# Second product of a Strassen feed-forward kernel transposed: weight sums stationary, 512 tokens moving

## The chip, the cores and the metric

The kernel runs on one core of one Trainium2 chip. The metric is the device time of one execution in microseconds. The engines that matter are TensorE (PE for matmuls, PEld for loading the stationary operand), VectorE (DVE), ScalarE (ACT) and SyncE (SP), which issues nearly all DMAs from one queue, in order.

## The reference

A retention layer (linear attention with a decaying state) feeds a two-layer network without bias:

```
state = gamma * state + k_t outer v_t;   y_t = q_t . state / sqrt(64)      # 4 batches, 8 heads, 768 steps
x = y as [3072 tokens, 512]
h = x @ w_in                # [3072, 2048]
g = h * clip(h + 3, 0, 6) / 6
out = g @ w_out             # [3072, 512]
```

All arrays are 32-bit floats. Each matmul operand is split into a high part in the reduced format fp32r and a low remainder, and a product takes three matmuls: high times high, high times low, low times high.

## The kernel before

The first part computes the retention and the first product, six groups of 512 tokens (u = 0 to 5) by sixteen pieces of the inner dimension of 128 each (jj). Its matmuls (L335) keep a 128x128 piece of w_in stationary and move 512 tokens, so h comes out transposed, inner dimension on the partitions. ACT (L339) and DVE (L340) make g, and SP writes it to arrays gd in the chip's main memory (L341), one array for each pair of inner pieces, 256 KB a time.

The second part is g @ w_out by one level of Strassen's method, in Winograd's form: seven products instead of eight. The quadrants of g are the two halves of a group of 256 tokens by the two halves of the inner dimension. For each of twelve groups (tb), four chunks (cf) of the inner dimension load the four quadrants (L398, two DMAs of 256 KB), DVE makes four sums of 128x256 (L86, L89), and `split` makes the high parts on ACT (L133) and the remainders on DVE (L134), seven operands together, held in `gc`. The sums of w_out, `w2c`, are made once, during the first part. The matmuls (L421) keep a 128x128 piece of `gc` stationary and move 256 columns of `w2c`; the seven products stand in four banks of the accumulator memory. At a group's end a chain of seven additions (L436) combines them into `ot`, which SP stores.

Raw quadrants (`gr`) have four buffers and `gc` four, two of each in either of two pools. TensorE's order in the first part is written by hand; in the second part, and on all other engines, a planner orders the instructions by its own estimate of when each can run, and queues then run strictly in that order. The first chunk's loads and splits have high priority; the other chunks of the first group may not be issued before the first part's last g.

Of the kernel before, what the change touches and what calls it, by code (L numbers as in the profile page):

```python
# [9 lines left out]
F32 = mybir.dt.float32  # L10
F32R = mybir.dt.float32r
# [3 lines left out]
AF = mybir.ActivationFunctionType  # L15
ALU = mybir.AluOpType
# [3 lines left out]
P = 128  # L20
SIXTH = 1.0 / 6.0

LEFT = {1: 0, 2: 1, 3: 2, 4: 3, 5: 4, 6: 5, 7: 6}
RIGHT = {1: 0, 2: 1, 3: 2, 4: 3, 5: 4, 6: 5, 7: 6}


# [1 line left out]
def retention_ffn(ctx: ExitStack, tc: tile.TileContext, qkv, w_in, w_out, dvs, dqs, out, B, H, S, D):  # L30
# [4 lines left out]


    nc = tc.nc
    NT, DM = out.shape
    NF = w_in.shape[0]
    NFP = NF // 2  # L40
    NPAIR = H // 2
# [3 lines left out]
    UR = 4  # L45
    UT = UR * P
    NU = NROW // UR
    HM = DM // 2
    WARM = 14
    AHEAD = 2 * UR  # L50
    WITH = (0, 2, 3, 5)
# [4 lines left out]
    NSLOT = 10  # L56
# [4 lines left out]
    dram = ctx.enter_context(tc.tile_pool(name="dram", bufs=1, space=DRAM))  # L61
    wpool = ctx.enter_context(tc.tile_pool(name="wpool", bufs=NSLOT))

    gd = [dram.tile([P, 2, NT], F32, name=f"gd{j}") for j in range(NFP)]

    cst_sb = const.tile([P, ROWS_B, H], F32, name="cst_sb")
    nc.scalar.dma_start(out=cst_sb.rearrange("p n h -> p (n h)"), in_=dvs)
# [5 lines left out]
        out=mask, in_=mask, pattern=[[1, P]], compare_op=ALU.is_ge, fill=0.0, base=0, channel_multiplier=-1  # L73
# [58 lines left out]
    def split(hi, lo, src):  # L132
        nc.scalar.activation(out=hi, in_=src, func=AF.Copy)  # L133
        nc.vector.tensor_tensor(out=lo, in0=src, in1=hi, op=ALU.subtract)  # L134
# [24 lines left out]
    w2c = {}  # L159
# [26 lines left out]
    xs, rows, before, early = {}, {}, {}, {}  # L186
# [143 lines left out]
    def mm1(u, jj):  # L330
        h = ps_h.tile([P, UT], F32, tag="h", name=nm("h"))
        for k in range(NK):
            t, o = w1_block(jj, k)
            for n, (a, b) in enumerate(((0, 0), (0, 1), (1, 0))):
                nc.tensor.matmul(  # L335
                    h, t[:, o, a], xs[u][b][:, k], start=k + n == 0, stop=(k, n) == (NK - 1, 2), skip_group_check=True
                )
        g = hpool.tile([P, UT], F32, tag="g", name=nm("g"))
        nc.scalar.activation(out=g, in_=h, func=AF.Relu, bias=three)  # L339
        ins = nc.vector.scalar_tensor_tensor(out=g, in0=g, scalar=6.0, in1=h, op0=ALU.min, op1=ALU.mult)  # L340
        nc.sync.dma_start(out=gd[jj // 2][:, jj % 2, u * UT : (u + 1) * UT], in_=g)  # L341
# [29 lines left out]
    ph1.close()  # L371


    sets = (late, ctx.enter_context(tc.tile_pool(name="gcpool", bufs=1, reuse_waits="tile")))
    gpool = ctx.enter_context(tc.tile_pool(name="gpool", bufs=2, reuse_waits="tile"))
    ps_o = [
        ctx.enter_context(tc.tile_pool(name=f"ps_o{i}", bufs=1, space=PSUM, reuse_waits="tile", side=side))
        for i, side in enumerate(("right", "left"))
    ]
    CF = 2  # L380

    for tb in range(NT // (2 * P)):
        t0 = tb * 2 * P
        banks = [ps_o[tb % 2].tile([P, 512], F32, tag=f"o{i}", name=f"o{tb}_{i}") for i in range(4)]
        acc = {}
        for b_, ids in enumerate(((1, 2), (6, 7), (5, 3), (4,))):
            for n, i in enumerate(ids):
                acc[i] = (banks[b_][:, n * HM : (n + 1) * HM], n == 0)
        for cf in range(NFP // CF):
            pool = sets[cf % 2]  # L390
            with ExitStack() as first:
                if tb == 0 and cf < 1:
                    first.enter_context(tc.high_priority())
                elif tb == 0:
                    first.enter_context(tc.issue_after(end))
                gv = pool.tile([P, CF, 2, 2, P], F32, tag="gr", name=f"gr{tb}_{cf}", bufs=2)
                for jj in range(CF):
                    nc.sync.dma_start(  # L398
                        out=gv[:, jj].rearrange("p f t n -> p f (t n)"),
                        in_=gd[cf * CF + jj][:, :, t0 : t0 + 2 * P],  # L400
                    )
                a11, a12, a21, a22 = gv[:, :, 0, 0, :], gv[:, :, 1, 0, :], gv[:, :, 0, 1, :], gv[:, :, 1, 1, :]
                sm = pool.tile([P, 4, CF, P], F32, tag="gsum", name=f"gsum{tb}_{cf}")
                dve_add(sm[:, 1], a21, a22)
                dve_sub(sm[:, 2], sm[:, 1], a11)
                dve_sub(sm[:, 3], a11, a21)
                dve_sub(sm[:, 0], a12, sm[:, 2])
                gc = pool.tile([P, 2, 7, CF, P], F32R, tag="gc", name=f"gc{tb}_{cf}")
                for i, src in ((0, a11), (1, a12), (3, a22)):
                    split(gc[:, 0, i], gc[:, 1, i], src)  # L410
                split(gc[:, 0, 4:7], gc[:, 1, 4:7], sm[:, 1:4])
                split(gc[:, 0, 2], gc[:, 1, 2], sm[:, 0])
            order = [(jj, i) for jj in range(CF) for i in (1, 2, 6, 7, 5, 3, 4)]
            if t0 + 2 * P == NT and cf == NFP // CF - 1:
                order.sort(key=lambda ji: (1, 2, 6, 7, 5, 3, 4).index(ji[1]))
            for jj, i in order:
                j = cf * CF + jj
                wc = w2c[j]
                ps, first = acc[i]
                for n, (a, b_) in enumerate(((0, 0), (0, 1), (1, 0))):  # L420
                    nc.tensor.matmul(  # L421
                        ps,
                        gc[:, a, LEFT[i], jj, :],
                        wc[:, RIGHT[i], b_],
                        start=first and j == 0 and n == 0,
                        stop=j == NFP - 1 and n == 2,
                        skip_group_check=True,
                    )
        ot = gpool.tile([P, 2, DM], F32, tag="ot", name=f"ot{tb}")
        p1 = gpool.tile([P, HM], F32, tag="op1", name=f"op1_{tb}")  # L430
        u2 = gpool.tile([P, HM], F32, tag="ou2", name=f"ou2_{tb}")
        u3 = gpool.tile([P, HM], F32, tag="ou3", name=f"ou3_{tb}")
        u4 = gpool.tile([P, HM], F32, tag="ou4", name=f"ou4_{tb}")

        def acc6(out_, i, other, s=SIXTH):
            nc.vector.scalar_tensor_tensor(out=out_, in0=acc[i][0], scalar=s, in1=other, op0=ALU.mult, op1=ALU.add)  # L436

        nc.scalar.activation(out=p1, in_=acc[1][0], func=AF.Copy, scale=SIXTH)
        acc6(ot[:, 0, :HM], 2, p1)
        acc6(u2, 6, p1)  # L440
        acc6(u3, 7, u2)
        acc6(ot[:, 1, HM:], 5, u3)
        acc6(u4, 5, u2)
        acc6(ot[:, 0, HM:], 3, u4)
        acc6(ot[:, 1, :HM], 4, u3, -SIXTH)
        rows = out[t0 : t0 + 2 * P, :].rearrange("(t p) m -> p t m", p=P)
        if t0 + 2 * P < NT:
            nc.sync.dma_start(out=rows, in_=ot)
# [63 lines left out]
```

## Time and profile before

| | us |
|---|---|
| median of 3 runs | 609.75 (608.75 to 611.29) |
| profiled execution: its own time is given as its span, first to last instruction | 608.6 |
| first matmul of the second product | 365.05 |
| last matmul starts | 604.65 |
| matmuls of the first product (128x512 moving) | 1152 |
| matmuls of the second product (128x256 moving) | 2016 |
| DMA traffic over the span | 104.07 MB |

The rows of a group read: line, engine, operation, output and inputs, shape, count, then busy time and mean duration of one, then the idle time before them and who ended it. Matmuls overlap in the pipeline, so the time that one costs is read from the distance of many starts, not from its duration.

### The profile page before, as it was taken

The numbers are of one execution on the slowest core, as the hardware profiler recorded it, in microseconds if no ns is written. First come the engines' busy times: TensorE is split into PE (matmuls) and PEld (weight loads), VectorE is DVE, ScalarE is ACT, GpSimd is POOL, SyncE is SP. The second block draws the span as 40 slices with busy tenths as digits, with TensorE's granted clock in tenths as the row PEclk, the third lists the DMA queues.
The fourth block names the chain that finished last, engine by engine and source line by source line (L and its number), as shares of the span: only waits on it lengthen the run. The fifth ranks groups of instructions, "written<-read, shape, count | busy, mean of one in ns | idle before, by whom it ended". The sixth has DMA issues, their size and how long they took to land.

```text
span 608.6 us, 11524 instructions
## 1 busy us (share of the span) xinstructions
PE 594.1 (98%) x4444; PEld 536.7 (88%) x4444; DVE 457.5 (75%) x960; ACT 258.6 (42%) x540; POOL 20.1 (3%) x24
## 2 busy tenths in 40 slices
PE   7699999999999999999999999999999999999997
PEld 6586888888888888888888889999999999999997
DVE  4879999999333596333336979988898889988983
ACT  6764454544222353222224544444444444444441
POOL 0001000000100010000000000000000000000000
PEclk9989999999999999999999999999999999999999
DMA  8965677666644467455334426443444344434411
GB/s 324 389 234 191 226 248 260 207 209 225 217 164 156 156 208 258 148 165 173 124 122 155 173 97 198 139 127 117 139 139 139 105 139 139 139 104 140 143 66 36
DMA packets 64728, 104.07 MB, mean 171 GB/s; under 512 B 5793, under 2 KB 30881, under 8 KB 64673
## 3 DMA queue, kind: packets, MB, share of 16 engines
q1 hardware_dynamic: 64528, 103.31, 50.7%
q8 instruction: 35, 0.57, 0.4%
q14 instruction: 21, 0.16, 0.1%
q10 hardware_dynamic: 144, 0.02, 0.0%
HBM read 71.85 MB, written 31.46 MB: 170 GB/s over the span
## 4 chain that ended last, share of the span: by engine, by line
PE 76%; DVE 17%; DMA 4%; issue 2%; ACT 0%; SPq 0%; DVEq 0%
PE o L421 39%; PE h L335 30%; DVE we L124 2%; DVE g L340 2%; PE y L249 2%; PE sc L245 2%; DVE wb L121 2%; DVE w L134 2%; DVE am L286 2%; PE y L238 2%; DMA early<-in_qkv 2%; DVE ww L127 2%; DVE x L134 1%; DVE xr L264 1%; DMA early<-in_decays_y 1%
## 5 line engine op out<-in xcount | busy, mean ns | idle before, releaser
L335 PE MATMUL h<-x,w 128*128 128x512 f32 x1152 | 270.1, 393 | 3.7 <-ACT x L133 2.5
L335 PEld LDWEIGHTS h<-x,w 128*128 128x128 f32 x1152 | 215.1, 188 | 51.4 <-ACT x L133 3.0
L421 PEld LDWEIGHTS o<-w,gc 128*128 128x128 f32 x2016 | 239.9, 191 | 0.1
L421 PE MATMUL o<-w,gc 128*128 128x256 f32 x2016 | 239.9, 282 | 0.0
L340 DVE SCALAR_TENSOR_TENSOR g<-g,h 128x512 f32<-128x512 f32 x96 | 65.6, 684 | 84.2 <-ACT g L339 82.1
L339 ACT ACTIVATE g<-h,three 128x512 f32<-128x512 f32 x96 | 65.6, 686 | 105.7 <-PE h L335 102.9
L133 ACT ACTIVATE gc<-gr 128x256 fp32r<-128x256 f32 x144 | 49.6, 408 | 118.5 <-PE o L421 114.2
L134 DVE TENSOR_TENSOR gc<-gr,gc 128x256 fp32r<-128x256 f32 x144 | 52.7, 421 | 20.1 <-ACT gc L133 20.1
L134 DVE TENSOR_TENSOR gc<-gsum,gc 128x768 fp32r<-128x768 f32 x96 | 62.0, 688 | 5.6 <-ACT gc L133 5.6
L133 ACT ACTIVATE gc<-gsum 128x768 fp32r<-128x768 f32 x96 | 54.6, 617 | 0.1
L133 ACT ACTIVATE w<-ww 128x384 fp32r<-128x384 f32 (+2 forms) x34 | 18.7, 556 | 43.6 <-DVE ww L127 41.1
L286 DVE TENSOR_TENSOR am<-sc,mask 128x1024 f32<-128x1024 f32 x24 | 29.2, 1215 | 0.0
L119 ACT ACTIVATE we<-we,ebias 128x512 int32<-128x512 int32 x32 | 23.0, 717 | 14.4 <-DVE we L115 14.3
L216 POOL TENSOR_TENSOR vn<-vn,cst_sb 128x512 f32<-128x512 f32 x16 | 19.3, 1209 | 272.6 <-DMA vn<-in_qkv 228.8
L127 DVE SCALAR_TENSOR_TENSOR ww<-wb,we 128x512 f32<-128x512 f32 x32 | 22.5, 704 | 0.7
L134 DVE TENSOR_TENSOR w<-ww,w 128x384 fp32r<-128x384 f32 (+2 forms) x34 | 20.8, 617 | 2.7 <-ACT w L133 2.6
L124 DVE SCALAR_TENSOR_TENSOR we<-st,we 128x512 int32<-128x512 int32 x32 | 22.8, 711 | 0.0
L89 DVE TENSOR_TENSOR gsum<-gr 128x256 f32<-128x256 f32 x48 | 20.4, 425 | 2.7 <-DMA gr<-gd 1.1
L121 DVE SCALAR_TENSOR_TENSOR wb<-st,wb 128x512 f32<-128x512 uint32 x32 | 22.0, 687 | 0.2
L115 DVE TENSOR_SCALAR we<-st 128x512 int32<-128x512 int32 x32 | 14.4, 449 | 9.0 <-DMA st<-in_w_in 8.7
L282 ACT ACTIVATE state<-uz 128x512 f32<-128x512 f32 x20 | 11.8, 591 | 21.7 <-PE uz L273 21.7
L86 DVE TENSOR_TENSOR gsum<-gr,gsum 128x256 f32<-128x256 f32 x48 | 20.2, 421 | 0.7
(50 smaller groups left out, 375.9 us busy)
## 6 DMA issues: line engine op xcount, KB each, us to landing
gd<-g SPq DMA_DIRECT2D x96, 256.0 KB, 2.3
gr<-gd SPq DMA_DIRECT2D x96, 256.0 KB, 3.2
st<-in_w_in SPq DMA_DIRECT2D x16, 512.0 KB, 4.5
st<-in_w_out SPq DMA_DIRECT2D x16, 512.0 KB, 3.7
early<-in_qkv SPq DMA_DIRECT2D x28, 256.0 KB, 6.0
out<-ot SPq DMA_DIRECT2D x11, 512.0 KB, 2.8
kn<-in_qkv SPq DMA_DIRECT2D x16, 256.0 KB, 5.1
kt<-in_qkv SPq DMA_DIRECT2D x16, 256.0 KB, 4.7
```

The source lines that it names most:

```text
L89: nc.vector.tensor_tensor(out=out_, in0=a, in1=b, op=ALU.add)
L119: nc.scalar.activation(out=e, in_=e, func=AF.Relu, scale=8.0, bias=ebias)
L121: nc.vector.scalar_tensor_tensor(out=y, in0=lo.bitcast(U32), scalar=2.0**-32, in1=b, op0=ALU.mult, op1=ALU.add)
L124: nc.vector.scalar_tensor_tensor(out=e, in0=hi, scalar=-2147483648, in1=e, op0=ALU.bitwise_and, op1=ALU.bitwise_or)
L127: nc.vector.scalar_tensor_tensor(out=w, in0=y, scalar=2.0**-20, in1=e.bitcast(F32), op0=ALU.mult, op1=ALU.mult)
L133: nc.scalar.activation(out=hi, in_=src, func=AF.Copy)
L134: nc.vector.tensor_tensor(out=lo, in0=src, in1=hi, op=ALU.subtract)
L286: nc.vector.tensor_tensor(out=new["am"].rearrange("p h a n -> p (h a) n"), in0=sc.rearrange("p h a n -> p (h a) n"), in1=mask[:, None, :]. ...
L335: nc.tensor.matmul(h, t[:, o, a], xs[u][b][:, k], start=k + n == 0, stop=(k, n) == (NK - 1, 2), skip_group_check=True)
L339: nc.scalar.activation(out=g, in_=h, func=AF.Relu, bias=three)
L340: ins = nc.vector.scalar_tensor_tensor(out=g, in0=g, scalar=6.0, in1=h, op0=ALU.min, op1=ALU.mult)
L421: nc.tensor.matmul(ps, gc[:, a, LEFT[i], jj, :], wc[:, RIGHT[i], b_], start=first and j == 0 and n == 0, stop=j == NFP - 1 and n == 2, ski ...
```

## The change

The second product is turned round. The stationary operand is now a 128x128 piece of the sums of w_out, and the moving one is 512 tokens of an operand of g. The output comes out transposed ([512, 3072]) and the host's return statement transposes it back. The Strassen quadrants are now the two groups of 512 tokens in a block of 1024 by the two inner halves: three blocks (b). The seven products, each with two halves h of 128 output columns, would need fourteen banks, so each block goes through the inner dimension four times (sweeps s = 0 to 3) with products (1, 2), (6, 7), (5, 3) and (4); sweeps use the two sets of four banks in turn.

A step is one inner pair j in one sweep (in the last sweep, two). It loads what its sweep needs: s = 0 both quadrants of the first tokens (one DMA of 512 KB), s = 1 three quadrants (256 KB and 512 KB), s = 2 one (256 KB), s = 3 two (256 KB each). That is seven quadrants loaded where it was four. Sweep 1 makes three sums, of which the first two stay in `keep` for sweep 2, which makes the fourth. Every step splits two operands of 128x512 and has twelve matmuls. Raw data have two buffers for each of three kinds (`gr` for sweeps 0 and 3, `gr2`, `gr3`), `gc` four. Additions at a sweep's end replace the chain at a group's end. The layout of gd puts a group of 512 tokens together.

```diff
-    gd = [dram.tile([P, 2, NT], F32, name=f"gd{j}") for j in range(NFP)]
+    gd = [dram.tile([P, NU, 2, UT], F32, name=f"gd{j}") for j in range(NFP)]
...
-        nc.sync.dma_start(out=gd[jj // 2][:, jj % 2, u * UT : (u + 1) * UT], in_=g)
+        nc.sync.dma_start(out=gd[jj // 2][:, u, jj % 2], in_=g)
...
+    SWEEPS = ((1, 2), (6, 7), (5, 3), (4,))
+    NB = NU // 2
+    work = [(b, s, j) for b in range(NB) for s in range(4) for j in range(0, NFP, 1 + (s == 3))]
...
+    def load_g(step):
+        b, s, j = step
+        if s == 1:
+            t = rest.tile([P, 3, UT], F32, tag="gr2", name=nm("gr2"), bufs=2)
+            nc.sync.dma_start(out=t[:, 0], in_=gd[j][:, 2 * b, 0])
+            nc.sync.dma_start(out=t[:, 1:3], in_=gd[j][:, 2 * b + 1])
+        elif s == 2:
+            t = rest.tile([P, UT], F32, tag="gr3", name=nm("gr3"), bufs=2)
+            nc.sync.dma_start(out=t, in_=gd[j][:, 2 * b, 1])
+        else:
+            t = late.tile([P, 2, UT], F32, tag="gr", name=nm("gr"), bufs=2)
+            if s == 0:
+                nc.sync.dma_start(out=t, in_=gd[j][:, 2 * b])
+            else:
+                for i in range(2):
+                    nc.sync.dma_start(out=t[:, i], in_=gd[j + i][:, 2 * b + 1, 1])
+        raws[step] = t
+
+    def sums(step):
...
+        if s == 1:
+            a11, a21, a22 = (t[:, i] for i in range(3))
+            s3 = rest.tile([P, UT], F32, tag="s3", name=nm("s3"), bufs=2)
+            dve_add(s1, a21, a22)
+            dve_sub(s2, s1, a11)
+            dve_sub(s3, a11, a21)
+            raws[step] = (s2, s3)
+        elif s == 2:
+            dve_sub(t, t, s2)
+            raws[step] = (s1, t)
...
+    def split_g(step, n):
+        t = raws.pop(step)
+        gc = (late, rest)[n // 2 % 2].tile([P, 2, 2, UT], F32R, tag="gc", name=nm("gc"), bufs=2)
+        if isinstance(t, tuple):
+            for i in range(2):
+                split(gc[:, i, 0], gc[:, i, 1], t[i])
+        else:
+            split(gc[:, :, 0], gc[:, :, 1], t)
+        gcs[step] = gc
+
+    def mm2(step, hs):
...
                 for n, (a, c) in enumerate(((0, 0), (0, 1), (1, 0))):
                     nc.tensor.matmul(
-                        gc[:, a, LEFT[i], jj, :],
-                        wc[:, RIGHT[i], b_],
+                        banks[b, i, h],
+                        w2c[jj][:, RIGHT[i], a, h],
+                        gc[:, q, c],
...
+    for n, step in enumerate(work):
...
+        with tc.issue_after(end):
+            for _ in range(NFP if last else 1):
+                prepare_next()
+                load_next()
+        if not last:
+            mm2(step, range(2))
+            if work[n + 1][1] != s:
+                for h in range(2):
+                    evict(b, s, h)
+            continue
```

The lines move by two in the first part: `split` is L131 and L132, the sums L84 and L87, loads L389 to L400, the matmul L443, stores L455, additions L460, the scaled copy L466. Instructions of the first part stand as before on every engine until near its end; three places of the second part follow.

**SyncE, before**, in steady state: loads of the raw quadrants `gr` of two chunks, then a group's store of `ot`.

```order
L398 DMA gr_0_4518<-gd_63 128x2x256
L398 DMA gr_0_4518<-gd_64 128x2x256
L448 DMA out<-ot_4238 128x2x512
L398 DMA gr_1_4579<-gd_65 128x2x256
L398 DMA gr_1_4579<-gd_66 128x2x256
```

**SyncE, now**, where the second block begins: `c` and `u` are output pieces of the first block (c_641, u_589 and their like from sweep 2; u_619 and u_620 from sweep 3), gr_4016 and the next `gr` are the raw data of the second block's sweep 0, gr_674 and gr_700 those of its later sweeps.

```order
L455 DMA out<-c_641_4001 128x512
L455 DMA out<-c_642_4007 128x512
L455 DMA out<-u_589_3637 128x512
L390 DMA gr_674_4228<-gd_66 128x1024
L455 DMA out<-u_591_3642 128x512
L397 DMA gr_4016<-gd_63 128x1024
L397 DMA gr_4035<-gd_64 128x1024
L393 DMA gr_700_4385<-gd_64 128x512
L397 DMA gr_4052<-gd_65 128x1024
L455 DMA out<-u_619_3833 128x512
L397 DMA gr_4069<-gd_66 128x1024
L455 DMA out<-u_620_3836 128x512
```

The first loads of a block's sweep 0 stand behind the stores of the block before, and each load is one of 128x1024 for one step.

**VectorE, before**, for one chunk (`gsum` are the sums; `gc` the operands):

```order
L134 TENSOR_TENSOR gc_1_3801<-gr_1_3793,gc_1_3801 128x256 x3
L134 TENSOR_TENSOR gc_1_3801<-gsum_1_3796,gc_1_3801 128x768
L134 TENSOR_TENSOR gc_1_3801<-gsum_1_3796,gc_1_3801 128x256
L89 TENSOR_TENSOR gsum_3_3918<-gr_3_3915 128x256
L86 TENSOR_TENSOR gsum_3_3918<-gr_3_3915 128x256
```

**VectorE, now**, over the same place (the end of sweep 2 and sweep 3 of the first block, then sweep 0 of the second):

```order
L460 SCALAR_TENSOR_TENSOR u_591_3642<-o_3859,u_591_3642 128x512
L132 TENSOR_TENSOR gc_4032<-gr_3986,gc_4032 128x2x512
L84 TENSOR_TENSOR keep_3464<-keep_3463,gr_671_4204 128x512
L84 TENSOR_TENSOR gr_697_4362<-gr_697_4362,keep_3464 128x512
L87 TENSOR_TENSOR keep_3463<-gr_674_4228 128x512
L84 TENSOR_TENSOR keep_3464<-keep_3463,gr_674_4228 128x512
L132 TENSOR_TENSOR gc_4049<-gr_4016,gc_4049 128x2x512
L460 SCALAR_TENSOR_TENSOR u_619_3833<-o_4018,u_619_3833 128x512
L132 TENSOR_TENSOR gc_4066<-gr_4035,gc_4066 128x2x512
L460 SCALAR_TENSOR_TENSOR u_620_3836<-o_4025,u_620_3836 128x512
L132 TENSOR_TENSOR gc_4087<-gr_4052,gc_4087 128x2x512
L132 TENSOR_TENSOR gc_4108<-gr_4069,gc_4108 128x2x512
```

Each step of sweep 0 has one remainder of 128x1024 on this engine; sums of the second block's sweep 1 (the `keep` rows) have been taken ahead into the first block's last sweeps.

More of the change, by code (lines that the diff above doesn't have):

```diff
@@ L21 @@
 SIXTH = 1.0 / 6.0
-LEFT = {1: 0, 2: 1, 3: 2, 4: 3, 5: 4, 6: 5, 7: 6}
 RIGHT = {1: 0, 2: 1, 3: 2, 4: 3, 5: 4, 6: 5, 7: 6}
@@ L37, in retention_ffn @@
     nc = tc.nc
-    NT, DM = out.shape
+    DM, NT = out.shape
     NF = w_in.shape[0]
@@ L47, in retention_ffn @@
     NU = NROW // UR
-    HM = DM // 2
     WARM = 14
@@ L371, in retention_ffn @@
     ph1.close()
-    sets = (late, ctx.enter_context(tc.tile_pool(name="gcpool", bufs=1, reuse_waits="tile")))
-    gpool = ctx.enter_context(tc.tile_pool(name="gpool", bufs=2, reuse_waits="tile"))
     ps_o = [
@@ L379, in retention_ffn @@
     ]
[L380 to L422, printed above, removed]
-                        gc[:, a, LEFT[i], jj, :],
-                        wc[:, RIGHT[i], b_],
-                        start=first and j == 0 and n == 0,
-                        stop=j == NFP - 1 and n == 2,
@@ new lines, in retention_ffn @@
+    rest = ctx.enter_context(tc.tile_pool(name="rest", bufs=1, reuse_waits="tile"))
+    keep = [wpool.tile([P, 7, UT], F32, tag="w", name=f"keep{i}", bufs=NSLOT - 1) for i in range(2)]
+    keep = [k[:, i] for k in keep for i in range(7)] + [rest.tile([P, UT], F32, name=f"keep_{i}") for i in range(2)]
+    SWEEPS = ((1, 2), (6, 7), (5, 3), (4,))
+    NB = NU // 2
+    work = [(b, s, j) for b in range(NB) for s in range(4) for j in range(0, NFP, 1 + (s == 3))]
+    raws, gcs, banks, outs = {}, {}, {}, {}
@@ new lines, in sums @@
+    def sums(step):
+        b, s, j = step
+        t = raws.pop(step)
+        s1, s2 = keep[j], keep[NFP + j]
+        if s == 1:
[9 more added lines that the diff above has]
+        else:
+            raws[step] = t
@@ new lines, in split_g @@
+    def split_g(step, n):
+        t = raws.pop(step)
+        gc = (late, rest)[n // 2 % 2].tile([P, 2, 2, UT], F32R, tag="gc", name=nm("gc"), bufs=2)
+        if isinstance(t, tuple):
+            for i in range(2):
+                split(gc[:, i, 0], gc[:, i, 1], t[i])
+        else:
+            split(gc[:, :, 0], gc[:, :, 1], t)
+        gcs[step] = gc
+    def mm2(step, hs):
+        b, s, j = step
+        gc = gcs[step]
+        for h in hs:
+            for q in range(2):
+                i = SWEEPS[s][q if s < 3 else 0]
+                jj = j if s < 3 else j + q
+                if (b, i, h) not in banks:
+                    banks[b, i, h] = ps_o[s % 2].tile([P, UT], F32, tag=f"o{2 * h + (q if s < 3 else 0)}", name=nm("o"))
+                for n, (a, c) in enumerate(((0, 0), (0, 1), (1, 0))):
+                    nc.tensor.matmul(
+                        banks[b, i, h],
+                        w2c[jj][:, RIGHT[i], a, h],
+                        gc[:, q, c],
+                        start=jj == 0 and n == 0,
+                        stop=jj == NFP - 1 and n == 2,
@@ L427, in retention_ffn @@
                         skip_group_check=True,
                     )
[L429 to L448, printed above, removed]
-        else:
-            for t in range(2):
-                for m in (slice(0, HM), slice(HM, DM)):
-                    nc.sync.dma_start(out=rows[:, t, m], in_=ot[:, t, m])
+    def store(b, mh, th, h, t, cols=slice(0, UT)):
+        m = (2 * mh + h) * P
+        t0 = (2 * b + th) * UT
+        nc.sync.dma_start(out=out[m : m + P, t0 + cols.start : t0 + cols.stop], in_=t[:, cols])
@@ new lines, in evict, with add @@
+    def evict(b, s, h, cols=(slice(0, UT),)):
+        def add(out_, i, other, f=SIXTH, cut=slice(0, UT)):
+            nc.vector.scalar_tensor_tensor(
+                out=out_[:, cut], in0=banks[b, i, h][:, cut], scalar=f, in1=other[:, cut], op0=ALU.mult, op1=ALU.add
+            )
+        if s == 0:
+            outs[h] = rest.tile([P, UT], F32, tag=f"u2_{h}", name=nm("u2"))
+            nc.scalar.activation(out=outs[h], in_=banks[b, 1, h], func=AF.Copy, scale=SIXTH)
+            c11 = rest.tile([P, UT], F32, tag="c11", name=nm("c11"), bufs=2)
+            add(c11, 2, outs[h])
+            store(b, 0, 0, h, c11)
+        elif s == 1:
+            outs[2 + h] = rest.tile([P, UT], F32, tag=f"u3_{h}", name=nm("u3"))
+            add(outs[h], 6, outs[h])
+            add(outs[2 + h], 7, outs[h])
+        elif s == 2:
+            c22 = rest.tile([P, UT], F32, tag="c22", name=nm("c22"), bufs=2)
+            add(c22, 5, outs[2 + h])
+            store(b, 1, 1, h, c22)
+            add(outs[h], 5, outs[h])
+            add(outs[h], 3, outs[h])
+            store(b, 1, 0, h, outs[h])
+        else:
+            for cut in cols:
+                add(outs[2 + h], 4, outs[2 + h], -SIXTH, cut)
+                store(b, 0, 1, h, outs[2 + h], cut)
@@ new lines, in retention_ffn, with load_next, prepare_next @@
+    SOON, FAR = 2, 4
+    loaded, ready = iter(work), enumerate(work)
+    def load_next():
+        step = next(loaded, None)
+        if step:
+            load_g(step)
+    def prepare_next():
+        n, step = next(ready, (0, None))
+        if step:
+            sums(step)
+            split_g(step, n)
+    with tc.high_priority():
+        for n in range(SOON):
+            load_next()
+            prepare_next()
+    with tc.issue_after(end):
+        for n in range(SOON, FAR):
+            load_next()
@@ new lines, in retention_ffn @@
+    for n, step in enumerate(work):
+        b, s, j = step
+        last = b == NB - 1 and s == 3
+        if last and j:
+            break
+        with tc.issue_after(end):
+            for _ in range(NFP if last else 1):
+                prepare_next()
+                load_next()
+        if not last:
[4 more added lines that the diff above has]
+            continue
+        for h in range(2):
+            for later in work[n:]:
+                mm2(later, (h,))
+            evict(b, s, h, (slice(0, UT),) if h == 0 else (slice(0, UT // 2), slice(UT // 2, UT)))
@@ L506 @@
     ]
-    out = nc.dram_tensor("out", (B * S, moe_w_out.shape[1]), F32, kind="ExternalOutput").ap()
+    out = nc.dram_tensor("out", (moe_w_out.shape[1], B * S), F32, kind="ExternalOutput").ap()
     with tile.TileContext(nc) as tc:
@@ L510 @@
     r = run_bass_kernel_spmd(nc, [arrays], core_ids=[0])
-    return r.results[0]["out"]
+    return np.ascontiguousarray(r.results[0]["out"].T)
```

## The prediction

> **What bounds the kernel now.** I read the page's busy shares first, then the chain of waits in order of time, then the windows of the second product, then groups and single stretches for prices.
>
> ```profile
> span 608.6 us, 11524 instructions
> ...
> PE 594.1 (98%) x4444; PEld 536.7 (88%) x4444; DVE 457.5 (75%) x960; ACT 258.6 (42%) x540; POOL 20.1 (3%) x24
> ...
> PEclk9989999999999999999999999999999999999999
> ```
>
> ```profile
> 316.02 49.19 PE h L335 x216
> 365.21 239.01 PE o L421 x2010
> ```
>
> ```profile
> 366.00:586.00 220.00, 220.00 (x1853) 220.00 (x1852) 194.90 (x480) 96.59 (x235) 0.00 (x0) 1.00 0.41 134
> ```
>
> TensorE is busy 98% of the span at full granted clock. The chain of waits is one unbroken run of L421 from 365.21 to 604.2, and in the window of the second product (columns: PE, PEld, DVE, ACT, POOL busy, clock, DMA share, GB/s) TensorE is busy 220.00 of 220 us. So the second product costs its count of matmuls times the distance between two starts, and nothing else. VectorE stands at 194.90 of 220, close behind, and is the engine to watch.
>
> **The gain: distance of starts.** The chain's 2010 matmuls of 256 columns in 239.01 us make 118.9 ns each. For 512 columns, the first product without the retention beside it, and the second product's end for comparison, in the timeline:
>
> ```profile
> 349.63 15.57 PE L335 MATMUL h<-x,w 128*128 128x512 f32 x68
> ...
> 589.74 15.19 PE L421 MATMUL o<-w,gc 128*128 128x256 f32 x126
> ```
>
> A stretch of n matmuls is n - 1 distances and one duration of some 0.39 (L335) or 0.28 us (L421):
>
> ```profile
> L335 PE MATMUL h<-x,w 128*128 128x512 f32 x1152 | 270.1, 393 | 3.7 <-ACT x L133 2.5 <-DVE x L134 1.1
> ...
> L421 PE MATMUL o<-w,gc 128*128 128x256 f32 x2016 | 239.9, 282 | 0.0
> ```
>
> (15.57 - 0.39) / 67 = 226.6 ns for 512 columns, and (15.19 - 0.28) / 125 = 119.3 for 256, in line with 118.9. The change makes 3 blocks x (3 sweeps x 8 steps + 4 steps) x 12 = 1008 matmuls of the very shape of L335: 128x128 stationary, 512 moving. Two of 256 cost 237.8, one of 512 costs 226.6: 11.2 ns less, times 1008 is **-11.3 us**. By the chain's own row for L335, 49.19 / 216 = 227.7, which includes the seam at its start, it is -10.2; I keep both ends.
>
> Here the Trainium skill speaks against the change. "TensorE: Matmul & The Clock Gate", section "Back-to-back issue gap", gives N/2.4 + 2.5 ns, so 109.2 for 256 and 215.8 for 512: by it two of 256 lose 2.5 ns against one of 512, and the gain would be 2.5 us. Both rows lie above it, by 9.7 and 10.8 ns; I go by the rows.
>
> **What VectorE and ScalarE have to do.** Elements stay the same (seven operands to split, four sums and seven additions for each piece of g); instructions get longer and fewer. Prices:
>
> ```profile
> L133 ACT ACTIVATE gc<-gr 128x256 fp32r<-128x256 f32 x144 | 49.6, 408 | 118.5 <-PE o L421 114.2 <-DMA gr<-gd 4.3
> L134 DVE TENSOR_TENSOR gc<-gr,gc 128x256 fp32r<-128x256 f32 x144 | 52.7, 421 | 20.1 <-ACT gc L133 20.1
> L134 DVE TENSOR_TENSOR gc<-gsum,gc 128x768 fp32r<-128x768 f32 x48 | 45.9, 957 | 5.6 <-ACT gc L133 5.6
> L133 ACT ACTIVATE gc<-gsum 128x768 fp32r<-128x768 f32 x48 | 39.9, 832 | 0.1
> ```
>
> ```profile
> 354.50 0.69 DVE L124 SCALAR_TENSOR_TENSOR we<-st,we 128x512 int32<-128x512 int32 x1
> 355.10 0.68 DVE L340 SCALAR_TENSOR_TENSOR g<-g,h 128x512 f32<-128x512 f32 x1
> 355.70 0.69 DVE L121 SCALAR_TENSOR_TENSOR wb<-st,wb 128x512 f32<-128x512 uint32 x1
> ```
>
> On VectorE, 512 columns follow each other at 0.60 us and last 0.69. A line through 256 and 768 gives 1.22 us for 1024 on VectorE (0.957 + 0.268) and 1.04 on ScalarE (0.832 + 0.212), and 0.62 there for 512. A block has 32 sums, 32 remainders of 512 (sweeps 1 and 2), 12 of 1024 at a distance of some 1.14, and 14 additions: (32 + 32 + 14) x 0.60 + 12 x 1.14 = 60.5 us, where TensorE has 336 x 0.2266 = 76.1. VectorE becomes freer on the whole. By sweep it isn't: sweep 1 has 3 sums and 2 remainders in a step, 3.0 us, against TensorE's 12 x 0.2266 = 2.72.
>
> **What is late next: raw data in two buffers.** Before, four `gr` buffers served chunks of 42 matmuls each (42 x 2 x 0.1189 = 10 us for two of them). Now each kind has two, for steps of 2.72 us, so a buffer has to come round in 5.44. A round is: remainder done, SP issues, data land, high part, remainder. Handoffs, at the last g of the first product:
>
> ```profile
> 365.25 0.69 ACT L339 ACTIVATE g<-h,three 128x512 f32<-128x512 f32 x1 [2.03 <-PE h L335]
> 365.97 0.69 DVE L340 SCALAR_TENSOR_TENSOR g<-g,h 128x512 f32<-128x512 f32 x1 [2.03 <-ACT g L339]
> ...
> 366.69 0.33 SPq L341 DMA_DIRECT2D gd<-g  x1
> ```
>
> ScalarE ends at 365.94, VectorE starts 0.03 later; it ends at 366.66 and SP issues 0.03 later. Landing, from SP's issue, for the fetches of w_out (512 KB) in the window 330 to 350, and for a lone decay load of 256 KB between 295 and 310:
>
> ```profile
> DMA to landing us min/median/max: 3.3/3.5/3.8
> ```
>
> ```profile
> DMA to landing us min/median/max: 2.5/2.5/2.5
> ```
>
> *Sweep 0*, 512 KB: 3.5 + 1.04 + 1.22 + three handoffs of some 0.04 = 5.9 (5.7 to 6.2), over 5.44 by 0.45 (0.25 to 0.75). In the first block the steps are prepared while the first product still runs, and the order puts matmuls of sweep 1 between. In the other two no lead is left at the start: SP's first loads of sweep 0 stand behind the stores of sweep 2, whose six additions and one remainder keep VectorE until about 4.9 us after that sweep's end; 3.5 to land, 1.04 and 1.22 make 10.7 to 11.3, and TensorE, four steps of sweep 3 later, asks at 10.9. So about 0.2 at the start and 4 rounds x 0.45, 2.0 us in each of two blocks: **+4.0** (2.0 to 6.6).
>
> *Sweep 1*, 768 KB: the step from 256 to 512 KB costs 1.0, so 4.5 to land, and three sums, 1.9: 6.4 over 5.44. Blocks 2 and 3 find the sums of four steps done (the `keep` rows of the order), which leaves 8 x 2 remainders, 4 x 3 sums, two late ones and two additions, 32 x 0.60 = 19.2 against 21.8: covered. Block 1 has three steps ahead; the last two or three come late: **+1.0** (0 to 3).
>
> *Sweep 2*, 256 KB: 2.5 + 0.69 + 0.62 + 0.69 + 0.1 = 4.6, within 5.44, but the sums taken ahead for the next block stand between on VectorE at 0.60 each: **+0.6** for three (0 to 3).
>
> *Sweep 3* loads as much as sweep 0 in a step, but of its four steps two are loaded before it begins, so it has one round only, and lead for it: nothing.
>
> **At nothing:** the seam between the products (two steps prepared ahead, 24 x 0.2266 = 5.4 us, cover the two splits, 2.26 each, that wait for the last g's engines); the doubled accumulator use (sweeps alternate, a set is free for a whole sweep before it comes again; cover gone it would cost the additions, 1.2 to 3.6 us a sweep); the larger traffic as such (7 quadrants for 4); the end. Of the last matmuls the old kernel adds and stores pieces of 128x256, and so does the new one:
>
> ```profile
> 604.96 0.76 DVE L436 SCALAR_TENSOR_TENSOR ot<-o,ou 128x256 f32<-128x256 f32 x2
> ```
>
> From there to the span's end are 3.6 us in both; a lost cover there is at most 0.5.
>
> **Sum:** -11.3 + 4.0 + 1.0 + 0.6 = -5.7 against the span of 608.6, so 602.9. The median of the runs is 1.1 above that span: **604.0**. All at their best: 609.75 - 11.3 + 2.0 = 600.4, and with no stall at all 598.5. All at their worst: -10.2 + 6.6 + 3 + 3 = +2.4, 612.2.
>
> **Rivals.** (a) *No stall shows*, since VectorE runs ahead further than I counted or loads land at 3.3 and less: 598.5 (up to 600.5). For it: the order lets sweep 1 be prepared early. Against: the order of SP's queue above. (b) *Stalls eat the gain*: sweeps 0 and 2 both run at their buffers' pace. With 4.0 us to land instead of 3.5 sweep 0 costs 0.95 x 8 + 0.4 = 8, sweep 2 some 0.4 x 9 = 3.6 with VectorE's other work, sweep 1 1.5: +13 - 11.3, about 611. For it: loads under traffic took longer:
>
> ```profile
> st<-in_w_in SPq DMA_DIRECT2D x16, 512.0 KB, 4.5
> ...
> kt<-in_qkv SPq DMA_DIRECT2D x16, 256.0 KB, 4.7
> ```
>
> against: at most one or two loads are in flight, at 4 MB in 21.8 us. (c) *Slower*: the same round in sweep 0, at 4.5 to land, is 6.9, so 1.45 x 8 = 11.6 there, and the later kinds go with it, 9 x 0.65 = 5.9 in sweep 2 and 3 in sweep 1: +20.5 - 11.3, about 619. It decides from a landing of some 4.2. (d) *The 512 columns bring nothing*: the first product's 226.6 is due to its own order (twelve matmuls into one bank, where L443 changes bank every three), and here two times 118.9 stays. Then there is no gain, two steps last 5.71, and sweep 0 costs 0.2 x 8 + 0.4 = 2.0, sweep 1 some 0.5: 612.2. For it: the second product is the only one that changes banks; against: it is TensorE alone that would have to lose 11 ns, in a stream that waits for nothing. By the Trainium skill's rule above the gain would be 2.5 instead, so 609.7; the two rows that lie 10 ns above it speak against that.
>
> **Chances.** Forecast, 600.5 to 606.5: 0.50. (a) 0.22. (b) 0.16. (c) 0.07. (d) 0.05. A measurement tells 0.5%, 3 us, from no change: faster is below 606.7, so the forecast and (a), 0.72; within it (b) and (d), up to 612.8, 0.21; slower (c), 0.07. The range takes (a) in and reaches half-way into (b): 598.3 to 609.8.
>
> **What would show it.** L443 with 1008 matmuls at 226 to 228 ns where nothing stalls. TensorE idle before L443 on VectorE's L132, some 4 us in sweeps 0 of the second and third block (from some 443 and 521), in pieces of under 1 us, every second step, and little in sweep 0 of the first. VectorE's share in the second product down from 89% to some 78% (3 x 60.5 of 234). Wrong would be: distances near 237 ns (d); a gap at the seam of the two products; TensorE waiting mostly in sweeps 1 or 2; or PEclk below 9.

## Result: slower by half a per cent

| | before | after |
|---|---|---|
| median of 10 runs, us | 610.61 (607.81 to 611.41) | 613.41 (611.56 to 614.94) |
| ratio | | 1.0054, 95% interval 1.0037 to 1.0070 |
| span of the profiled execution, us | 608.6 | 609.8 |
| first to last start of the second product, us | 365.05 to 604.65: 239.6 | 364.14 to 605.70: 241.6 |

The kernel became slower by 2.8 us; 604.0 was forecast, with a range that ended at 609.8. The profiled execution after took 611.56 us, the shortest of its ten, so its trace shows 1.2 us of the 2.8; the others have no trace. The page after:

```profile
span 609.8 us, 9211 instructions
...
PE 589.7 (97%) x3436; PEld 485.7 (80%) x3436; DVE 433.5 (71%) x715; ACT 249.6 (41%) x426; POOL 20.6 (3%) x24
...
PEclk8989999999999999999999999999999999999999
...
DMA packets 55916, 122.79 MB, mean 201 GB/s; under 512 B 6336, under 2 KB 6592, under 8 KB 55872
...
L443 PE MATMUL o<-gc,w 128*128 128x512 f32 x1008 | 235.1, 393 | 6.8 <-DVE gc L132 6.5
...
L131 ACT ACTIVATE gc<-gr 128x1024 fp32r<-128x1024 f32 (+1 forms) x60 | 52.7, 886 | 91.0 <-DMA gr<-gd 60.7
...
gr<-gd SPq DMA_DIRECT2D x48, 512.0 KB, 4.6
gr<-gd SPq DMA_DIRECT2D x72, 256.0 KB, 3.2
```

The matmuls of the second product, L443, now have idle time before them, 6.8 us; before, L421 had 0.0. VectorE's remainder (L132) ends it, but VectorE isn't short of time: the same window that held 194.90 us of its work before now holds 173.50.

```profile
366.00:586.00 220.00, 214.49 (x922) 171.71 (x921) 173.50 (x254) 87.69 (x130) 0.00 (x0) 1.00 0.67 209
```

What is late is behind it: ScalarE's high part (L131) waited 60.7 us for raw data. The chain of waits (start, length, what) is no longer one run of matmuls. From the second block on it hops between loads, high parts and remainders:

```profile
445.36 4.92 DMA gr<-gd
451.48 1.24 DVE gc L132
452.73 4.19 DMA gr<-gd
458.12 1.24 DVE gc L132
459.38 3.85 DMA gr<-gd
...
515.76 5.39 DMA gr<-gd
522.32 1.24 DVE gc L132
523.58 3.78 DMA gr<-gd
...
543.79 44.04 PE o L443 x191
...
591.67 3.98 DMA gr<-gd
...
599.12 6.98 PE o L443 x29
```

One such round in the timeline, at the start of the second block's sweep 0:

```profile
445.36 0.32 SPq L397 DMA_DIRECT2D gr<-gd  x1
...
450.39 1.06 ACT L131 ACTIVATE gc<-gr 128x1024 fp32r<-128x1024 f32 x1 [1.19 <-DMA gr<-gd]
...
450.51 2.85 PE L443 MATMUL o<-gc,w 128*128 128x512 f32 x11 [0.76 <-DVE gc L132]
451.48 1.23 DVE L132 TENSOR_TENSOR gc<-gr,gc 128x1024 fp32r<-128x1024 f32 x1 [1.02 <-ACT gc L131]
```

Issued at 445.36, landed by 450.28 (the chain's 4.92), high part until 451.45, remainder until 452.71, and at 452.73 SP may issue into this buffer again: 7.37 us for a round that serves two steps, 24 x 0.2292 = 5.50 of TensorE's time. The next, to 459.38, takes 6.65. The two are 1.87 and 1.15 too long, 3.0 together; TensorE lost 2.96 in this sweep.

Where TensorE waits for nothing, a stretch of n matmuls gives the distance of starts, as in the prediction:

```profile
469.82 52.41 PE L443 MATMUL o<-gc,w 128*128 128x512 f32 x228
```

(52.41 - 0.39) / 227 = 229.2 ns, not 226.6. The whole second product is then 1007 x 0.2292 = 230.8 of matmuls and 10.8 of waits. By sweep (starts further apart than that distance, summed): sweep 0 of blocks 1, 2, 3: 0, 2.96, 3.72; sweep 1: 2.04, 0, 0; sweep 2: 0.35, 0, 0; sweep 3: 0, 0, 1.72.

### The profile page after: what moved, and what is told of

It reads as the page before. It is cut to its first block, busy times and chain, and to the rows that moved or that the text cites. A ratio compares the mean times of both kernels' runs of the same rounds, so it can differ in the third digit from the quotient of the medians.

```text
span 609.8 us, 9211 instructions
## 1 busy us (share of the span) xinstructions
PE 589.7 (97%) x3436; PEld 485.7 (80%) x3436; DVE 433.5 (71%) x715; ACT 249.6 (41%) x426; POOL 20.6 (3%) x24
## 4 chain that ended last, share of the span: by engine, by line
PE 49%; DVE 27%; DMA 16%; issue 3%; ACT 3%; SPq 1%; DVEq 0%; ACTq 0%
PE h L333 30%; DMA gr<-gd 13%; PE o L443 12%; DVE gc L132 6%; DVE g L338 2%; ACT gc L131 2%; PE y L247 2%; PE sc L243 2%; DVE we L122 2%; DMA st<-in_w_in 2%; DVE wb L119 2%; DVE am L284 2%; DVE w L132 2%; PE y L236 2%; DVE ww L125 2%
## 5 line engine op out<-in xcount | busy, mean ns | idle before, releaser
L443 PE MATMUL o<-gc,w 128*128 128x512 f32 x1008 | 235.1, 393 | 6.8 <-DVE gc L132 6.5
L443 PEld LDWEIGHTS o<-gc,w 128*128 128x128 f32 x1008 | 187.9, 188 | 53.9 <-DVE gc L132 12.0
L131 ACT ACTIVATE gc<-gr 128x1024 fp32r<-128x1024 f32 (+1 forms) x60 | 52.7, 886 | 91.0 <-DMA gr<-gd 60.7
L132 DVE TENSOR_TENSOR gc<-gr,gc 128x1024 fp32r<-128x1024 f32 (+1 forms) x60 | 60.0, 1008 | 36.4 <-ACT gc L131 36.0
L131 ACT ACTIVATE gc<-keep 128x512 fp32r<-128x512 f32 x48 | 29.7, 624 | 25.3 <-DVE keep L84 13.2
L131 ACT ACTIVATE w<-ww 128x384 fp32r<-128x384 f32 (+2 forms) x34 | 18.7, 555 | 43.8 <-DVE ww L125 41.3
L132 DVE TENSOR_TENSOR gc<-keep,gc 128x512 fp32r<-128x512 f32 x48 | 32.5, 685 | 1.0 <-ACT gc L131 1.0
L117 ACT ACTIVATE we<-we,ebias 128x512 int32<-128x512 int32 x32 | 22.9, 717 | 14.2 <-DVE we L113 14.2
L460 DVE SCALAR_TENSOR_TENSOR u<-o,u 128x512 f32<-128x512 f32 (+1 forms) x31 | 20.1, 666 | 5.8 <-PE o L443 5.8
L131 ACT ACTIVATE gc<-s 128x512 fp32r<-128x512 f32 x24 | 15.0, 625 | 20.9 <-DVE s L84 20.9
L87 DVE TENSOR_TENSOR keep<-gr 128x512 f32<-128x512 f32 x24 | 16.5, 688 | 9.3 <-DMA gr<-gd 9.2
L132 DVE TENSOR_TENSOR w<-ww,w 128x384 fp32r<-128x384 f32 (+2 forms) x34 | 19.9, 592 | 2.7 <-ACT w L131 2.6
```

What stands on the lines that cost most here:

```text
L117: nc.scalar.activation(out=e, in_=e, func=AF.Relu, scale=8.0, bias=ebias)
L443: nc.tensor.matmul(banks[b, i, h], w2c[jj][:, RIGHT[i], a, h], gc[:, q, c], start=jj == 0 and n == 0, stop=jj == NFP - 1 and n == 2, skip_ ...
L460: nc.vector.scalar_tensor_tensor(out=out_[:, cut], in0=banks[b, i, h][:, cut], scalar=f, in1=other[:, cut], op0=ALU.mult, op1=ALU.add)
```

## The experiments

Each was compared with the kernel before on the same chip. As one measure of the second product in all of them I use the busy and idle time of its matmuls' group: 235.1 + 6.8 = 241.9 us in the changed kernel.

### Four raw buffers instead of three times two

```diff
+        n = next(count)
+        t = (late if n < 4 or n // 2 % 2 else rest).tile([P, 3, UT], F32, tag="raw", name=nm("raw"), bufs=2)
         if s == 1:
-            t = rest.tile([P, 3, UT], F32, tag="gr2", name=nm("gr2"), bufs=2)
...
-            t = rest.tile([P, UT], F32, tag="gr3", name=nm("gr3"), bufs=2)
+            t = t[:, 0]
...
-            t = late.tile([P, 2, UT], F32, tag="gr", name=nm("gr"), bufs=2)
+            t = t[:, 0:2]
```

All sweeps share one kind of buffer, `raw`, of which there are four, two in each pool. Loads, splits and matmuls are the same; the sums c11 and c22 share their two buffers to make room.

> The three kinds of raw buffers (two each of 4, 6 and 2 KB a partition) become four of 6 KB that all kinds share; the two pairs of output pieces c11 and c22 share two buffers to make room. Theory A (a round of a raw buffer, landing plus high part plus remainder or sums, is longer than the two steps that two buffers give it): with four buffers a round has four steps, 10.9 us, and nearly all of the 10.5 us of stalls go: 613.4 - 8.5, so 603 to 606, and TensorE waits under 3 us for L132's successor. Theory B (the stores that stand ahead of the loads in SyncE's queue start them late): stalls at the starts of sweeps stay, 609 to 612. Theory C (VectorE and ScalarE are too slow in some sweeps): no change, 612 to 615.

Measured: 602.20 us (600.62 to 602.42), ratio 0.9866 (0.983 to 0.9901). Groups and DMA issues:

```profile
L446 PE MATMUL o<-gc,w 128*128 128x512 f32 x1008 | 231.2, 392 | 0.0
...
L131 ACT ACTIVATE gc<-raw 128x1024 fp32r<-128x1024 f32 (+1 forms) x60 | 53.1, 886 | 63.8 <-PE o L446 42.7
...
raw<-gd SPq DMA_DIRECT2D x48, 512.0 KB, 5.2
```

TensorE waits for nothing any more, though the loads take longer to land (5.2 us instead of 4.6). ScalarE now waits for TensorE to release `gc`, where it waited for data. So neither the traffic nor the landing as such costs the time, but the landing inside a round of two buffers. The group is 10.7 us shorter, and the kernel some 11 by the medians (613.41 and 602.20), 0.8 below the range that I had given for theory A.

### Stores on another queue

```diff
-        nc.sync.dma_start(out=out[m : m + P, t0 + cols.start : t0 + cols.stop], in_=t[:, cols])
+        nc.gpsimd.dma_start(out=out[m : m + P, t0 + cols.start : t0 + cols.stop], in_=t[:, cols])
```

> All stores of the second product are issued from GpSimd's queue instead of SyncE's; nothing else. Theory A: the round of the buffers is the same, only the starts of sweep 0 in blocks 2 and 3 gain: 611 to 613.5. Theory B: the loads no longer wait behind stores, most of the stalls go: 604 to 607. Theory C: no change.

Measured: 615.30 us (614.41 to 615.98), ratio 1.0088 (1.0057 to 1.0118).

```profile
L443 PE MATMUL o<-gc,w 128*128 128x512 f32 x1008 | 237.3, 396 | 5.9 <-DVE gc L132 4.4 <-ACT gc L131 1.5
```

That is 1.9 us more than the changed kernel, where all three theories had the same time or less. The group takes 243.2 instead of 241.9 us: the waits stay (5.9 us for 6.8) and shift to other sweeps, and some 1.6 us more go into eight matmuls of the third block that start 427 ns apart and not 229, at half the clock (shown under "Sweep 0's loads twice"). What the medians differ by beyond that lies outside the second product. Stores ahead of the loads in SP's queue are not what most of the waits come from.

### Sweep 0 without loads in the second and third block

```diff
+            if s == 0 and b:
+                raws[step] = fixed[0]
+                return
+            if step == (0, 0, 2):
+                fixed.append(late.tile([P, 2, UT], F32, name="fixed"))
...
```

As with the four raw buffers, c11 and c22 share their two buffers here, to make room for the resident tile.

> Sweep 0 of blocks 2 and 3 loads nothing and splits one resident raw tile again and again (its products are then of the wrong tokens: this leaves out 16 loads of 512 KB). ScalarE, VectorE and TensorE do the same work. Theory A: the 2.9 and 3.7 us of stalls in those two sweeps go, the others (sweep 1 of block 1, the last sweep) stay: 613.4 - 6.5, so 606 to 608. Theory B: the same or less, since the late start goes too, but stalls inside the sweep would stay: 609 to 611. Theory C: no change, the two sweeps still stall.

Measured: 603.10 us (602.40 to 604.06), ratio 0.9890 (0.986 to 0.9919).

```profile
L451 PE MATMUL o<-gc,w 128*128 128x512 f32 x1008 | 232.5, 392 | 0.8 <-DVE gc L132 0.6 <-ACT gc L131 0.2
```

With every conversion still done but 16 loads gone, the group is 8.6 us shorter (233.3), and the sweeps 0 of blocks 2 and 3 have no wait: there ScalarE and VectorE alone keep up with TensorE. Sweep 1 of the first block still waits 1.9 us. I had expected 606 to 608. Part of the surplus is the wait in the last sweep, 1.7 us, which went too. That isn't because sweep 0 left the buffers of that sweep free: in the changed kernel, too, the first two steps of sweep 3 had their data by 549.90. But there their high parts stood in ScalarE's queue behind the last one of sweep 2 and began at 586.94, 6.2 us before the sweep's first matmul; here they began at 578.01, 8.0 us before. Why sweep 2 was further ahead here stays open. The rest is about the 1.85 us by which the changed kernel's median lies above its profiled execution; no trace shows it.

### Sweep 0's loads twice

```diff
             if s == 0:
-                nc.sync.dma_start(out=t, in_=gd[j][:, 2 * b])
+                for _ in range(2):
+                    nc.sync.dma_start(out=t, in_=gd[j][:, 2 * b])
```

> Every load of sweep 0 is issued twice, one behind the other, in all three blocks (same data twice). Theory A: landing of the pair is 0.8 to 1.6 us later, four rounds in each of blocks 2 and 3 are longer by that: 613.4 + 6 to 13, so 620 to 627. Theory B: only the first load of a sweep counts: 614 to 616. Theory C: no change.

Measured: 649.00 us (645.79 to 649.69), ratio 1.0631 (1.0591 to 1.067), much more than expected. The waits of SP's queue and a piece of the chain show why:

```profile
SPq L398 <- DMA gr<-gd: 46.2, 28, 5.0
```

```profile
470.73 3.54 DMA gr<-gd
...
474.33 4.22 DMA gr<-gd
...
478.66 1.07 ACT gc L131
```

In all 24 pairs the second load into a tile isn't issued until the first has landed, so the round grows by a whole landing, some 4 us, and not by the 0.8 to 1.6 that I had put for more traffic. As a measure of the price of traffic the run is void; as a test of the round it points the same way. But not all of the loss is waits:

```profile
L444 PE MATMUL o<-gc,w 128*128 128x512 f32 x1008 | 249.3, 409 | 28.9 <-ACT gc L131 26.6 <-DVE gc L132 2.2
```

Against the changed kernel that is 22.1 us more of waits and 14.2 more of matmuls (235.1 there). The window and the timeline show what slowed them:

```profile
456.00:491.00 35.00, 28.15 (x95) 21.39 (x96) 12.49 (x13) 8.66 (x10) 0.00 (x0) 0.83 0.69 211
```

```profile
466.86 7.51 PE L444 MATMUL o<-gc,w 128*128 128x512 f32 x24 [2.80 <-ACT gc L131]
```

```profile
460.98:467.81 6.83, 4.03 (x18) 2.86 (x16) 0.97 (x1) 1.06 (x1) 0.00 (x0) 1.00 0.72 223
467.81:471.22 3.41, 3.41 (x9) 2.48 (x8) 1.48 (x2) 1.06 (x1) 0.00 (x0) 0.50 0.50 149
```

The granted clock is 0.83 in the mean from 456 to 491, but it is never that: it is 1.00 or, for 3.41 or 6.83 us at a time, 0.50, and there matmuls start 427 ns apart. The 24 matmuls behind the wait of 2.80 us take 7.51 us because eight of their 23 distances, 412 to 591 ns, fall into that stretch. The longest waits of the matmuls (sum, times, longest), of this run and of the changed kernel, where the clock of the second product is 1.00:

```profile
PE o L444 <- ACT gc L131: 26.6, 10, 4.6
```

```profile
PE o L443 <- DVE gc L132: 6.5, 9, 1.5
```

The Trainium skill, "TensorE: Matmul & The Clock Gate", section "What's actually happening", gives half the clock after an idle window of some 3.4 us. The traces agree with the half and with the 3.4 us. They don't show that TensorE has to be idle all that time: with the stores on another queue, where no wait of the second product is longer than 0.9 us, it was busy for 1.77 of 3.41 us, and the next 3.42 us ran at half.

```profile
538.88:542.29 3.41, 1.77 (x7) 0.91 (x6) 1.22 (x1) 1.94 (x2) 0.00 (x0) 1.00 0.25 101
542.29:545.71 3.42, 3.42 (x10) 2.66 (x9) 1.23 (x1) 0.18 (x1) 0.00 (x0) 0.50 0.70 178
```

### All of `gc` in one pool, and all of it in the other

In the changed kernel steps take their `gc` in turn from two places: two buffers of each pool. The distances repeat with period four: 230.2, 228.9, 230.8 and 226.7 ns. The first run keeps the `gc` of all steps but the first two in the pool `rest` (the raw data go to `late`, in `gc`'s place there); the second keeps three `gc`, not four, in `late` (and the raw data in `rest`). Both are built on the kernel with four raw buffers.

```diff
-        gc = (late, rest)[n // 2 % 2].tile([P, 2, 2, UT], F32R, tag="gc", name=nm("gc"), bufs=2)
+        gc = (rest if n > 1 else late).tile([P, 2, 2, UT], F32R, tag="gc", name=nm("gc"), bufs=4 if n > 1 else 2)
```

```diff
-        gc = (late, rest)[n // 2 % 2].tile([P, 2, 2, UT], F32R, tag="gc", name=nm("gc"), bufs=2)
+        gc = late.tile([P, 2, 2, UT], F32R, tag="gc", name=nm("gc"), bufs=3)
```

> As the four shared raw buffers, but all gc buffers of steps 2 and later lie in one pool (byte addresses 149408 to 182176 of a partition) and the raw buffers in the other; until now gc alternated between the two pools. Distances of starts of L443 were 226.7 ns on average in one step of four, and 228.9 to 230.8 in the other three. If the extra 2.5 ns come from where gc lies or from the change of pool, all steps come to 226.7: 602.2 - 2.5, so 599 to 600. If they have another cause, such as the changes of bank every three matmuls, nothing changes: 602.

> As the four shared raw buffers, but three gc buffers, all in the pool at the upper addresses (204768 to 229344), and the raw buffers of steps 3 and later in the other pool. If the change of pool between steps costs the 2.5 ns, the distances come to 226.7 ns here too. If the upper region itself is the slow one, they come to 229 or more in every step. The time is 600 to 606 either way, as three gc buffers give less lead.

Measured: in `rest` 601.97 us (600.25 to 603.31), ratio 0.9866 (0.9842 to 0.989); in `late` 602.53 (601.64 to 603.59), ratio 0.9874 (0.9852 to 0.9896). The first has 226.7 ns in every step of the second and third block, and some 3 us of waits in the first, which took it past the 599 to 600 that I had expected; that the raw buffers come free later there is tested below. The second has the other distance (and 1.2 us beyond the sum of them):

```profile
522.66 18.70 PE L449 MATMUL o<-gc,w 128*128 128x512 f32 x81
```

(18.70 - 0.39) / 80 = 228.9 ns. So it matters where the moving operand lies: `rest` has it at bytes 149408 to 182176 of a partition, `late` at 204768 to 229344. But that is not all. With both places in turn the mean is 229.2, more than either place by itself, where half of each would make 227.8. The rest, 1.4 ns a matmul, goes with the change: the first step after a change to `late` has 230.2 and the next one there 228.9; the first after a change to `rest` has 230.8 and the next one there 226.7. The place of the raw data isn't behind it: in the changed kernel they lie in `late` in sweep 0 and in `rest` in sweep 1, with the same four distances. Why place and change matter I can't say.

### 256 columns in the turned order

The kernel with four raw buffers, each matmul of 512 columns as two of 256:

```diff
+                    for half in range(2):
+                        cut = slice(half * UT // 2, (half + 1) * UT // 2)
...
-                        banks[b, i, h],
+                            banks[b, i, h][:, cut],
...
-                        gc[:, q, c],
+                            gc[:, q, c, cut],
```

> As the four shared raw buffers, but every matmul of 512 columns is issued as two of 256 with the same stationary piece: 2016 matmuls as before the change, same data. By the rows of the kernel before (118.9 ns at 256) TensorE takes 2016 x 118.9 instead of 1008 x 229.2, +8.7: 610 to 612. By a fixed cost of 2.5 ns a matmul +2.5: 604.7. If the gain lies in the transposition itself and not in the 512 columns: 602.

Measured: 610.24 us (609.04 to 612.03), ratio 1.0004 (0.9988 to 1.002).

```profile
L448 PE MATMUL o<-gc,w 128*128 128x256 f32 x2016 | 240.0, 281 | 0.0
```

119.0 ns each, as before the change (118.9), and no wait: the kernel takes the time of the one before. Turning the product is worth nothing by itself; the 512 columns are worth 8.8 us of the group and 8.0 of the median.

### Four raw buffers, two of them in a shorter round

The kernel with four raw buffers, taken in another order:

```diff
-        t = (late if n < 4 or n // 2 % 2 else rest).tile([P, 3, UT], F32, tag="raw", name=nm("raw"), bufs=2)
+        t = (rest if n >= 4 and n % 3 == 1 else late).tile([P, 3, UT], F32, tag="raw", name=nm("raw"), bufs=2)
```

This isn't the three buffers that the expectation speaks of. There are still four, two in each pool; those in `late` serve two steps of three and so come round every three steps, those in `rest` every six.

> As the four shared raw buffers, but three of them. Theory A (the round): three buffers give a round 8.2 us where landing 4.4 to 5.5, high part and remainder, or sums, need 6.9 to 7.4, so the stalls stay away except in the last sweep, where a step has 1.4 us: 602 to 605. If four buffers helped by something else than the round, for instance by an order that the planner made differently, three may lie anywhere up to 613.

Measured: 603.04 us (601.61 to 604.41), ratio 0.9882 (0.9856 to 0.9909).

```profile
L446 PE MATMUL o<-gc,w 128*128 128x512 f32 x1008 | 233.5, 393 | 1.5 <-DVE gc L132 1.3 <-ACT gc L131 0.2
```

The time is inside the range, but it is no time of three buffers. What it shows is that a round of three steps is still too short in places: the group takes 235.0 us, 3.8 more than with the same four buffers in rounds of four steps. The waits are not in the last sweep, where I had expected them, but in sweep 1 of the first and third block, where a step loads 768 KB and makes three sums.

### Both: `gc` in one place, and enough raw buffers from the start

As `gc` in `rest`, and three steps of the first block take buffers for their raw data that the output pieces don't need yet:

```diff
+        if 4 <= n < 7:
+            tags = (("c", "c"), ("u2_0", "u2_1"), ("u3_0", "u3_1"))[n - 4]
+            raws[step] = tuple(rest.tile([P, UT], F32, tag=x, name=nm("raw"), bufs=1 + (x == "c")) for x in tags)
```

> The gc buffers of steps 2 and later in one region and four shared raw buffers, as in the run before, and steps 4 to 6 of the first block read their raw data into six buffers of the output pieces that are still free there (two DMAs of 256 KB each). If the 3.2 us of stalls left in the first block came from raw buffers that were free too late, they go, and TensorE takes 1008 x 226.7 = 228.5 without a stall: 598 to 600. If VectorE sets the pace of sweep 1 of the first block, about half of them stays: 600 to 602.

Measured: 598.08 us (597.01 to 598.54) against 609.93 before the change, ratio 0.9804 (0.9784 to 0.9823).

```profile
L455 PE MATMUL o<-gc,w 128*128 128x512 f32 x1008 | 228.8, 389 | 0.0
```

```profile
469.79 52.52 PE L455 MATMUL o<-gc,w 128*128 128x512 f32 x231
```

(52.52 - 0.39) / 230 = 226.7 ns and no wait: the group is 228.8 us where it was 239.9 before the change, 11.1 less, and the kernel is 11.85 faster. It is the fastest of all.

## Why the prediction was wrong

It forecast a gain of 11.3 us and stalls of 5.6; the runs show a gain of 8.7 and stalls of 10.8. What stalls, and by what mechanism, was said rightly but for the last sweep; the sizes were wrong, the landing in sweep 0's round above all.

**The bound** was read rightly: the second product costs its matmuls times the distance of starts as long as nothing stalls and the clock stays full. Every run here obeys it; those without waits differ only by distance.

**The gain** was forecast as 11.3 us and is 8.7 (1008 x (237.8 - 229.2) ns). The mechanism is right, as the run with 256 columns shows, and the price is right where `gc` lies in `rest` alone: 226.7 ns against the forecast 226.6. That the operand's place costs 2.2 ns in every second pair of steps, and the change of place 1.4 ns in the mean, was not in the sum. The alternative ends were less good: 227.7 ns is still short of 229.2; and rival (d) named the change of banks after every three matmuls, while `gc` in `rest` runs at 226.7 with just that order. By the formula of the Trainium skill ("TensorE: Matmul & The Clock Gate", section "Back-to-back issue gap") the gain would have been 2.5 us, an estimate. That section gives the formula for an isolated matmul, and some 131 ns for 512 columns in a stream of weight loads and matmuls; none of the averages here is below 226.6.

**Sweep 0** is the step that failed most: +4.0 forecast, 6.7 measured, in the two blocks and with the mechanism that were named. Its size came from a landing of 3.5 us, the median of the two fetches of w_out that fell into 330 to 350 us. Under the traffic of the changed second product (DMA share 0.67 in the window above, 0.41 before the change) the loads of sweep 0 take a median of 4.5 (3.8 to 6.3):

```profile
DMA to landing us min/median/max: 3.8/4.5/6.3
```

The rows that rival (b) quoted, 4.5 and 4.7 for loads under traffic, were the ones to use. Rival (c) had a landing of 4.5 and with it 619; that was too much, since it charged four long rounds to each block in full. In the second block two carry the excess. In the third the chain has four, from 515.76 to 543.79, 6.0 us more than four times 5.50, but TensorE lost 3.72 of it. And the sweeps 2 stall 0.35 in all, where it gave them 5.9. In time the result is (b)'s, 611 forecast and 613.4 measured, by sweep 0 and the last sweep rather than sweeps 0 and 2.

**Sweep 1** (+1.0, 2.0 measured, in the first block as said, inside its bounds of 0 to 3) and **sweep 2** (+0.6, 0.35 measured) were near.

**Sweep 3** was set at nothing, because two of its four steps are loaded before it begins; it cost 1.7, in the last block alone. The kernel's very last sweep runs all four steps for the first half of the output and then all four for the second, so a step is asked for after 6 matmuls, 1.4 us, and not 12. In the timeline:

```profile
593.82 1.06 ACT L131 ACTIVATE gc<-gr 128x1024 fp32r<-128x1024 f32 x1 [4.85 <-DMA gr<-gd]
...
595.76 1.06 ACT L131 ACTIVATE gc<-gr 128x1024 fp32r<-128x1024 f32 x1 [0.88 <-DMA gr<-gd]
...
597.26 0.68 DVE L460 SCALAR_TENSOR_TENSOR u<-o,u 128x512 f32<-128x512 f32 x1
...
597.86 1.22 DVE L132 TENSOR_TENSOR gc<-gr,gc 128x1024 fp32r<-128x1024 f32 x1
...
599.12 1.21 PE L443 MATMUL o<-gc,w 128*128 128x512 f32 x4 [1.29 <-DVE gc L132]
```

The last high part waits for data until 595.76, and its remainder then stands behind additions in VectorE's queue until 597.86. This order was in the program's text, and I did not look there for a shorter time per step.

**At nothing** were put rightly: the seam (no gap), the accumulators, the tail, and the traffic as such, as the four raw buffers show. VectorE's share fell to 173.50 / 220 = 79%, 78 forecast.

Added up in the profiled execution: the terms sum to -8.7 + 6.7 + 2.0 + 0.35 + 1.7 = +2.1 where -5.7 was forecast; the product's own ends say +2.0. It starts 0.9 us earlier, which I can't attribute; over all runs that start varies from 362.8 to 366.4. The 1.6 us by which the medians differ beyond the two spans are not in any trace; that waits vary with the landings from execution to execution is likely, but only argued.

## What to carry to other kernels

When work is cut into shorter steps, compare the round of a buffer (landing, conversions, the issue of the next load) with the steps that its buffers cover; nearly 11 us of gain hung on two buffers instead of four, while ScalarE and VectorE had time to spare. Take the landing from many loads of the same size at the traffic that the changed stage will have, not from two, and ask in every loop, the last one above all, how many matmuls there are before the next step is wanted. A gain per matmul that is a small difference of two large numbers (237.8 - 226.6 ns) shrinks by a quarter when one of them grows by 1% (229.2).

## What the runs showed of the hardware

- The distance of 128x512 matmuls with a new stationary operand each depends on where the moving operand lies: 226.7 ns at bytes 149408 to 182176 of a partition, 228.9 at 204768 to 229344. When pairs of steps take turns, the step after a change is slower than its successor in the same place (230.8 and 226.7, 230.2 and 228.9), and the mean is 229.2. In the kernel before, where `gc` is the stationary operand and each chunk takes it from the other place, the distance alternates by chunk too, 117.8 and 120.0 ns.
- Landing grows with what is in flight, by more than I allowed: two loads of 512 KB took 3.3 and 3.8 us before the change (DMA share 0.42 from 330 to 350 us), the 48 of the changed kernel 4.6 in the median (share 0.67 in the second product), and the same 48 took 5.2 when four buffers let more of them run at once. Where buffers suffice, that costs nothing: TensorE's idle time was 0.0.
- A second load into the same tile, with no other use between, was issued only once the first had landed, in all 24 pairs; SP's queue stood in waits for loads 28 times there, 46.2 us in all, up to 5.0. SP waits on a semaphore before it issues, so this is an order that the program holds, and no limit of the queue that any run here shows.
- After stretches in which TensorE was busy for only part of the time, its granted clock fell to 0.50 for 3.41 us or twice that, and matmuls of 512 columns then started 427 ns apart instead of 229. No single long wait is needed: 1.77 us busy out of 3.41, with no wait above 0.9 us, was enough in one run. It doesn't always follow: 1.56 us busy out of 3.42 left the clock at 1.00 once (375.64 to 379.06 in the run with doubled loads), so no threshold can be read from these runs.
